# Two weight pairs held in PSUM: group 2's seventh chunk in place of group 1's

## The chip, the cores and the metric

The kernel runs on one core of a Trainium2 chip. The metric is the device time of one execution in microseconds. The kernel before takes 2106.07 us, the median of three runs (2104.05 to 2109.13).

## The reference

Two independent results stand side by side in the output. Part A is a gated long convolution over 2048 positions and 1024 channels: a short shift filter on k, a product with v, a convolution of length 2048 through the FFT, and a product with q. Part B is a transformer layer with a recurrent memory, and it takes most of the time:

```python
for s in range(64):                                   # 64 segments of 32 rows
    h = concat(mem, x[32*s : 32*s + 32])              # 8 + 32 rows, 1024 wide
    q, k, v = h @ Wq, h @ Wk, h @ Wv                  # 32 heads of 128
    p = softmax(masked(q @ k.T * 128 ** -0.5))        # mem rows see everything, the others the past
    o = (p @ v) @ Wo
    mem, out[s] = o[:8], o[8:]
```

Each segment needs the memory rows of the one before. The segments are therefore run in order, and every segment passes over all four weight matrices, 8 MB each in bfloat16.

## The kernel before, in words

**Preparation.** Up to about 388 us the kernel computes part A, and it also computes q, k and v of the 8 last rows of every segment, which the loop of part B reads back. In the loop, 32 rows (8 memory rows and 24 of x) go through the weights.

**Pairs.** The weights of part B are cut into 64 pairs of 512 KB, each [128, 2, 1024]. `("qk", g, i)` is the i-th of eight chunks of the model dimension for head group g of four, with Wq and Wk side by side. `("v", G, i)` is the same for one half of Wv, and `("o", g, i)` is two heads of Wo. In the text they are written qk0/2, v0/3 and o2/3; counting starts at 0, so group 2's seventh chunk is qk2/6 and the values' sixth chunk is v0/5.

Most pairs stay in on-chip memory for the whole loop (tiles `Wearly`, `Wqk`, `Wv`, `Wop`, `Wlate`, `Wo`). The table `STREAM` (line 40) names 17 pairs that do not fit and are loaded again in every segment. Two further pairs are kept in PSUM as bfloat16, in the tiles `park`. The table `PARKED` (line 41) names them as its values.

**The ring.** Streamed and parked pairs are used from a ring of five buffers, `wring`. When the matmuls of a ring pair have been written, `done` (line 768) gives its place to something new. Normally that is `place` (line 686): the next streamed pair in the order of use is loaded by a DMA on SP's queue (line 691). If the consumed pair is a key of `PARKED`, the place goes to the parked pair instead, and the copy is put on a list. `unpark` (line 759) then writes the copies of that list into the programs of two engines: one half on ACT (line 762), one on DVE (line 763). So the call of `unpark` sets behind which ACT and DVE work the copies stand. All places are tracked by semaphores: the load or the copy starts when the old pair's matmuls have ended.

**One segment**, in the order written out by hand (lines 948 to 1032), as PE runs it:

- q and k of group 0 (`qk_part`, line 787); in it, after chunk 4, the first `unpark`
- v chunks 0 to 3 of the first half (`v_part`, line 803), group 0's transposes (`tr_a`, line 825), then `unpark`
- q and k of group 1, chunks 0 to 3; `scores` and `softmax` of group 0; chunks 4 to 7
- v chunks 4 to 7 of the first half, group 1's transposes, `v_out` (line 814: ACT copies the values out of PSUM into `vsb`)
- q and k of group 2, with scores and softmax of group 1 in the middle; `pv` (line 896: probabilities times values) of group 0
- the same for group 3, then v of the second half with the remaining scores and softmaxes
- `wo` (line 911) of groups 0 to 3 with `pv` of groups 2 and 3 between them; the memory rows of the result, transposed, become the next segment's `hT`

Each softmax is a chain that alternates between DVE and ACT: `mx` and the subtraction on DVE (lines 866, 867), two exponentials on ACT (875, 876), sum, reciprocal, product, transpose on DVE (879 to 884), and four copies into `PB` (`blocks`, line 887).

**Queues.** All loads of the ring stand on SP's queue in the order of the calls of `place`, with the load of the next segment's `qkb`. POOL's queue has the outputs and two small loads, ACT's queue the next rows of x. After the loop the last output rows are computed in one pass (lines 1034 to 1052).

Of the kernel before, what the change touches and what calls it, by code (L numbers as in the profile page):

```python
# [21 lines left out]
def fused_kernel(ctx: ExitStack, tc, q, k, v, shift_k, ssm_k, ssm_D, outa, x, mem0, Wq, Wk, Wv, Wo, outb, n_seg):  # L22
# [14 lines left out]
    NS = 17  # L37
    scale = 128.0 ** -0.5
    RING = 5
    STREAM = {"qk": ((2, 4), (3,), (2, 6), (2, 6)), "v": ((0, 3, 5), (1, 5)), "o": ((2,), (1,), (0, 3), (2,))}  # L40
    PARKED = {("qk", 0, 4): ("v", 0, 2), ("v", 0, 3): ("qk", 1, 6)}

    msched = tc.manual_schedule()
    msched.__enter__()
# [10 lines left out]
    def keys(m, g, r):  # L55
        return [(m, g, i) for i in r]
# [3 lines left out]
    pairs += [key for g in range(4) for key in keys("o", g, range(4))]  # L60
    streamed = [key for key in pairs if key[2] in STREAM[key[0]][key[1]]]
    parked = list(PARKED.values())
    resident = [key for key in pairs if key not in streamed and key not in parked]
# [49 lines left out]
    def res_half(key, n):  # L113
        if key not in res:
            if key in early:
                res[key] = wide["t"][:, early.index(key)]
            else:
                res[key] = res_pool[key].tile([128, 2, 1024], BF, name=f"W{key[0]}{key[1]}_{key[2]}")
        nc.sync.dma_start(res[key][:, n, :], half_src(key, n))
        return res[key][:, n, :]  # L120
# [580 lines left out]
    def load_h(s):  # L701

        H_ = acte.tile([128, 256], BF, tag="qks", name="H")
        if s == 0:
            nc.gpsimd.dma_start(H_[0:32, :], mem0.rearrange("t (dq c) -> (t dq) c", dq=4))
            nc.gpsimd.dma_start(H_[32:128, :], x[0:24].rearrange("t (dq c) -> (t dq) c", dq=4))
        else:
            nc.scalar.dma_start(H_[:], x[32 * s - 8:32 * s + 24].rearrange("t (dq c) -> (t dq) c", dq=4))
        return H_
# [49 lines left out]
    def unpark():  # L759
        while to_copy:  # L760
            key, t = to_copy.pop(0)
            nc.scalar.copy(t[:, 0, :], park[key][0][:])  # L762
            nc.vector.tensor_copy(t[:, 1, :], park[key][1][:])  # L763
# [4 lines left out]
    def done(key):  # L768
        if key in res:
            return  # L770
        if key in PARKED:
            t = ring.tile([128, 2, 1024], BF, tag="wring", name="wring")
            placed[PARKED[key]] = [t[:]]
            to_copy.append((PARKED[key], t))
        else:
# [11 lines left out]
    def qk_part(u, kcs):  # L787
        if kcs[0] == 0:
            u.qk = ps_a.tile([128, 512], F32, tag="a", name="qkacc")
        for kc in kcs:  # L790
            w = pair(("qk", u.g, kc))
            for t in range(2):
                for c2 in range(2):
                    p0 = 32 * (2 * t + c2)
                    nc.tensor.matmul(u.qk[p0:p0 + 32, :], lhsT=hT[:, kc, :], rhs=w[:, t, c2 * 512:(c2 + 1) * 512],  # L795
                                     start=(kc == 0), stop=(kc == 7), tile_position=(0, p0))
            done(("qk", u.g, kc))

    def qk_out(u):
        u.qks = acte.tile([128, 512], BF, tag="qks", name="qks")  # L800
        nc.scalar.copy(u.qks[:], u.qk[:])  # L801

    def v_part(G_, kcs):
        if kcs[0] == 0:
            vacc[0] = ps_a.tile([128, 512], F32, tag="a", name="vacc")
        for kc in kcs:
            w = pair(("v", G_, kc))
            for c in range(4):
                nc.tensor.matmul(vacc[0][32 * c:32 * c + 32, :].rearrange("p (n x) -> p n x", n=2), lhsT=hT[:, kc, :],  # L809
                                 rhs=w[:, :, c * 256:(c + 1) * 256], start=(kc == 0), stop=(kc == 7),  # L810
                                 tile_position=(0, 32 * c))
            done(("v", G_, kc))

    def v_out():
        v = act.tile([128, 2, 256], BF, tag="vsb", name="vsb")
        nc.scalar.copy(v[:].rearrange("p n x -> p (n x)"), vacc[0][:])  # L816
        return v

    def transposes(src):
        tp = ps_ts.tile([128, 512], BF, tag="ts", name="tp")  # L820
        for j in range(4):
            nc.tensor.transpose(tp[:, j * 128:(j + 1) * 128], src[:, j * 128:(j + 1) * 128], ident[:])  # L822
        return tp

    def tr_a(u):
        tp = transposes(u.qks)
        tv = tp[:].rearrange("e (j t c r) -> e t c j r", j=4, t=2, c=2)
        QK = acte.tile([128, 8, 72], BF, tag="qks", name="QK")
        u.QT, u.KT = QK[:, :, 0:32], QK[:, :, 32:72]
        nc.gpsimd.tensor_copy(u.KT[:, :, 32:40], u.qkb.rearrange("e (h t r) -> e t h r", h=8, t=2)[:, 1])  # L830
        nc.scalar.copy(u.QT.rearrange("e (c j) r -> e c j r", c=2), tv[:, 0])  # L831
        nc.scalar.copy(u.KT[:, :, 0:32].rearrange("e (c j) r -> e c j r", c=2), tv[:, 1])
# [6 lines left out]
    def new_u(g):  # L839
        u = G()  # L840
        u.g = g
        u.qkb = qkb[:, g, :]
        return u
# [43 lines left out]
    def blocks(u, by):  # L887
        for c in range(4):
            r = slice(32 * c, 32 * c + 32)
            to, src = PB[r, :, c, :], u.PT[r, :, 0:40]  # L890
            if by[c] == "A":
                nc.scalar.copy(to, src)
            else:
                (nc.vector if by[c] == "D" else nc.gpsimd).tensor_copy(to, src)  # L894
# [45 lines left out]
    def new_hT():  # L940
        return acte.tile([128, 8, 32], BF, tag="hT", name="hT")
# [6 lines left out]
    for s in range(n_seg):  # L948
        last = s + 1 == n_seg
        def first_loads(g):  # L950
            for key in (n_o[g - 1:g] if s == 0 and g else ()):
                for n in range(2):
                    res_half(key, n)

        first_loads(0)
        us = [new_u(g) for g in range(4)]
        u0, u1, u2, u3 = us
        qk_part(u0, range(0, 5))
        unpark()
        qk_part(u0, range(5, 8))  # L960
        qk_out(u0)
        v_part(0, range(0, 4))
        tr_a(u0)
        unpark()
        first_loads(1)
        qk_part(u1, range(0, 4))
        S = scores(u0)
        softmax(u0, S)
        if s == 0:
            nc.vector.memset(PB[:], 0.0)  # L970
        blocks(u0, "DDDD")
        qk_part(u1, range(4, 8))
        qk_out(u1)
        v_part(0, range(4, 8))
        tr_a(u1)
        u0.v = u1.v = v_out()
        first_loads(2)
        qk_part(u2, range(0, 4))
        S = scores(u1)
        softmax(u1, S)  # L980
        if last:
            spare = [key for key in resident if key[0] != "o" and key[1] < 1 + (key[0] == "qk") and key not in early]
            for key, at in zip([key for key in streamed if key[0] == "o"], spare):
                nc.sync.dma_start(res[at][:], Wst[key])
                res[key] = res[at]
            for s0, s1 in ((0, 32), (32, s)):
                nc.sync.dma_start(OLs[:, s0:s1].rearrange("e s h r -> e (s h r)"),
                                  OLd[:, s0:s1].rearrange("e s x -> e (s x)"))
        qk_part(u2, range(4, 8))
        qk_out(u2)  # L990
        pv(u0, s)
        blocks(u1, "DDDD")
        first_loads(3)
        qk_part(u3, range(0, 2))
        tr_a(u2)
        qk_part(u3, range(2, 6))
        S = scores(u2)
        softmax(u2, S)
        qk_part(u3, range(6, 8))
        qk_out(u3)  # L1000
        v_part(1, range(0, 1))
        pv(u1, s)
        blocks(u2, "DDDD")
        v_part(1, range(1, 2))
        tr_a(u3)
        v_part(1, range(2, 5))
        S = scores(u3)
        if not last:
            H = load_h(s + 1)
            qkb = load_b(s + 1)  # L1010
        softmax(u3, S)
        v_part(1, range(5, 8))
        u2.v = u3.v = v_out()
        Y = ps_a.tile([128, 512], F32, tag="a", name="yacc")
        wo(u0, Y)
        pv(u2, s)
        blocks(u3, "DDAA")
        wo(u1, Y)
        wo(u2, Y)
        pv(u3, s)  # L1020
        if not last:
            hT = new_hT()
            h_rows(H, hT, 8)
        wo(u3, Y)
        Y_sb = act.tile([128, 256], BF, tag="P", name="Y_sb")
        nc.scalar.copy(Y_sb[:], Y[:, 0:256])  # L1026
        if not last:
            fill_mem(hT, Y_sb)
        for dq in range(4):
            nc.gpsimd.dma_start(outb[32 * s:32 * s + 24, dq * 256:(dq + 1) * 256], Y_sb[32 * dq + 8:32 * dq + 32, :])  # L1030
        if not last:
            load_vb(s + 1)
# [88 lines left out]
```

## Time and profile before

| | |
|---|---|
| median of three runs | 2106.07 us |
| the profiled execution's own time | 2093.32 us |
| its span, first to last instruction | 2091.5 us |
| granted clock of PE, mean over the span | 0.984 |
| PE busy | 1702.4 us (81%) |
| DVE, ACT, POOL busy | 1115.3, 908.7, 413.1 us |
| moved by DMA | 728.64 MB, mean 348 GB/s |
| loop of part B | about 388 to 2002 us of the span |
| one ring load, issue to landing (shortest, median, longest) | 4.0, 6.4, 9.4 us |
| copy of half a parked pair | 0.69 us on DVE, 1.02 us on ACT |

The page shows one execution. Times are counted in microseconds from the first instruction. A row of the timeline gives the start, the duration, the engine, the line of the kernel, the operation, the tile written and the tiles read. In square brackets stand the idle time of the engine just before and what ended it. PE's busy share says little by itself, since the ends of its pipelined matmuls are modelled. The share of busy time is also an average over stages with different limits, so the loop is read by single segments.

### The profile page before, as it was taken

What the parts mean: (1) busy time and instruction counts of PE and PEld (TensorE: products, weight loads), DVE (VectorE), ACT (ScalarE), POOL (GpSimd) and SP (SyncE); (2) the same over time, 40 slices, a digit from 0 to 9 for tenths busy, and PEclk for the clock granted to TensorE, in tenths of its full rate; (3) what the DMA queues carried; (4) which work ended last, traced back from release to release, by engine and by line L of the source; (5) the groups of instructions that cost most, each with busy time, mean ns of one, the idle gap of its engine ahead of it and who ended that gap; (6) DMA issues with size and microseconds to landing.
All of it is one profiled execution on the core that took longest, in us unless ns stands there. A gap on an engine that the chain in (4) does not pass through costs nothing. (4 is left out here: it accounts for less than half of the span.)

```text
span 2091.5 us, 73911 instructions
## 1 busy us (share of the span) xinstructions
PE 1702.4 (81%) x30484; PEld 894.2 (43%) x30514; DVE 1115.3 (53%) x3313; ACT 908.7 (43%) x2276; POOL 413.1 (20%) x1018
## 2 busy tenths in 40 slices
PE   5888987888788888888887878888888878888879
PEld 2433233444444444444444444444444444444449
DVE  6986833355555555555555555555555555555541
ACT  5556731244444444444444444444444444444430
POOL 2004730121111111111111111111212121111110
PEclk9999999999999999999999999999999999999999
DMA  6899989999999999999999999999999999999980
GB/s 236 282 346 362 343 287 381 352 377 372 356 375 368 365 360 370 372 366 375 358 368 353 367 358 372 359 377 358 371 358 378 363 352 351 374 370 379 368 337 23
DMA packets 266384, 728.64 MB, mean 348 GB/s; under 512 B 65007, under 2 KB 77183, under 8 KB 265277
## 3 DMA queue, kind: packets, MB, share of 16 engines
q1 hardware_dynamic: 239486, 686.65, 88.8%
q0 software_dynamic: 15520, 22.06, 3.3%
q10 hardware_dynamic: 11040, 15.21, 2.1%
q8 instruction: 239, 3.92, 0.7%
q14 instruction: 99, 0.81, 0.1%
HBM read 673.52 MB, written 56.56 MB: 349 GB/s over the span
## 5 line engine op out<-in xcount | busy, mean ns | idle before, releaser
L795 PE MATMUL qkacc<-Wqk,hT 128*32 128x512 bf16 x4096 | 338.5, 383 | 0.0
L795 PEld LDWEIGHTS <-hT 128*32 128x32 bf16 x8192 | 184.9, 96 | 236.3 <-issue 84.2
L916 PEld LDWEIGHTS <-OT 128*32 128x32 bf16 x8192 | 210.1, 96 | 109.5 <-issue 59.2
L795 PE MATMUL qkacc<-wring,hT 128*32 128x512 bf16 x2048 | 204.9, 389 | 31.3 <-DMA wring<-Wstqk 25.5
L763 DVE COPY wring<-park 128x1024 bf16<-128x1024 bf16 x128 | 88.6, 692 | 239.4 <-PE vacc L809 124.8
L875 ACT ACTIVATE P<-S 128x128 bf16<-128x128 f32 x256 | 71.1, 278 | 330.4 <-DVE S L867 244.3
L809 PE MATMUL vacc<-Wv,hT 128*32 128x512 bf16 x2560 | 209.8, 382 | 0.0
L809 PE MATMUL vacc<-wring,hT 128*32 128x512 bf16 x1536 | 154.7, 387 | 65.5 <-DMA wring<-in_B_Wv_dram 63.6
L809 PEld LDWEIGHTS <-hT 128*32 128x32 bf16 x4096 | 113.0, 95 | 184.4 <-issue 108.3
L762 ACT COPY wring<-park 128x1024 bf16<-128x1024 bf16 x128 | 130.7, 1021 | 138.9 <-PE qkacc L795 112.8
L894 DVE COPY PB<-P 32x160 bf16<-32x160 bf16 x896 | 172.9, 193 | 10.6
L879 DVE TENSOR_REDUCE sm<-P 128x4 f32<-128x256 bf16 x256 | 107.5, 420 | 128.6 <-ACT P L876 128.6
L831 ACT COPY QK<-tp 128x256 bf16<-128x256 bf16 x256 | 95.4, 373 | 185.7 <-PE tp L822 184.5
L795 PE MATMUL qkacc<-Wearly,hT 128*32 128x512 bf16 x2048 | 161.0, 391 | 18.4 <-DVE hT L936 17.9
L830 POOL COPY QK<-qkb 128x64 bf16<-128x64 bf16 x256 | 61.3, 239 | 564.5 <-PE tp L822 404.8
L916 PE MATMUL yacc<-wring,OT 128*32 128x256 bf16 x2520 | 126.7, 274 | 37.4 <-DMA wring<-Wsto 35.2
L905 ACT CAST OT<-otacc 128x256 bf16<-128x256 f32 x256 | 98.7, 386 | 130.4 <-PE otacc L901 130.4
L801 ACT CAST qks<-qkacc 128x512 bf16<-128x512 f32 x256 | 151.1, 590 | 4.2 <-PE qkacc L795 3.5
L1030 POOL DMA_DIRECT2D out_dram<-Y_sb x256 | 129.1, 511 | 84.8 <-ACT Y_sb L1026 82.8
L822 PE MATMUL tp<-ident,qks 128*128 128x128 bf16 x1024 | 102.4, 223 | 52.6 <-ACT qks L801 50.3
L866 DVE TENSOR_REDUCE mx<-S 128x4 f32<-128x160 f32 x256 | 83.2, 325 | 85.2 <-PE S L863 79.5
L901 PE MATMUL otacc<-PB,vsb 128*128 128x160 bf16 x512 | 97.6, 238 | 35.3 <-ACT vsb L816 35.3
(212 smaller groups left out, 2957.1 us busy)
## 6 DMA issues: line engine op xcount, KB each, us to landing
wring<-Wstqk SPq DMA_DIRECT2D x448, 512.0 KB, 6.2
wring<-in_B_Wv_dram SPq DMA_DIRECT2D x320, 512.0 KB, 6.7
wring<-Wsto SPq DMA_DIRECT2D x315, 512.0 KB, 6.3
SK<-s_sb SPq DMA_DIRECT2D x8, 1024.0 KB, 5.5
SU<-s_sb SPq DMA_DIRECT2D x8, 1024.0 KB, 8.9
QKBd<-stq ACTq DMA_DIRECT2D x4, 2048.0 KB, 9.5
Kg<-SK SPq DMA_DIRECT2D x16, 512.0 KB, 7.0
Ug<-SU SPq DMA_DIRECT2D x16, 512.0 KB, 8.3
```

Source lines behind the costliest of these rows:

```text
L762: nc.scalar.copy(t[:, 0, :], park[key][0][:])
L795: nc.tensor.matmul(u.qk[p0:p0 + 32, :], lhsT=hT[:, kc, :], rhs=w[:, t, c2 * 512:(c2 + 1) * 512], start=(kc == 0), stop=(kc == 7), tile_pos ...
L801: nc.scalar.copy(u.qks[:], u.qk[:])
L809: nc.tensor.matmul(vacc[0][32 * c:32 * c + 32, :].rearrange("p (n x) -> p n x", n=2), lhsT=hT[:, kc, :], rhs=w[:, :, c * 256:(c + 1) * 256 ...
L822: nc.tensor.transpose(tp[:, j * 128:(j + 1) * 128], src[:, j * 128:(j + 1) * 128], ident[:])
L831: nc.scalar.copy(u.QT.rearrange("e (c j) r -> e c j r", c=2), tv[:, 0])
L879: nc.vector.tensor_reduce(out=sm[:], in_=Pv.rearrange("p b x k -> p x b k"), op=ALU.add, axis=AX.XY)
L894: (nc.vector if by[c] == "D" else nc.gpsimd).tensor_copy(to, src)
L901: nc.tensor.matmul(o, lhsT=w[:, i * 128:(i + 1) * 128], rhs=PB[:, 2 * kb + i].rearrange("p c q -> p (c q)"), start=(kb == 0), stop=(kb == 1))
L905: nc.scalar.copy(u.OT[:].rearrange("e (c i) q -> e i c q", i=2), ov[:, :, :, 0:32])
L916: nc.tensor.matmul(Y[32 * dq:32 * dq + 32, 0:256], lhsT=u.OT[:, hh, 0:32], rhs=w[:, hh % 2, dq * 256:(dq + 1) * 256], start=(u.g == 0 and ...
L1030: nc.gpsimd.dma_start(outb[32 * s:32 * s + 24, dq * 256:(dq + 1) * 256], Y_sb[32 * dq + 8:32 * dq + 32, :])
```

## The change

Group 1's seventh chunk, qk1/6, which was kept in PSUM, becomes a streamed pair. Group 2's seventh chunk, qk2/6, which was streamed, is kept in PSUM. The number of streamed and of parked pairs stays the same. The parked pair's copy now takes the place of v0/5 in the ring (before, that of v0/3), and its `unpark` stands behind group 1's transposes (before, behind group 0's).

```diff
-    STREAM = {"qk": ((2, 4), (3,), (2, 6), (2, 6)), "v": ((0, 3, 5), (1, 5)), "o": ((2,), (1,), (0, 3), (2,))}
-    PARKED = {("qk", 0, 4): ("v", 0, 2), ("v", 0, 3): ("qk", 1, 6)}
+    STREAM = {"qk": ((2, 4), (3, 6), (2,), (2, 6)), "v": ((0, 3, 5), (1, 5)), "o": ((2,), (1,), (0, 3), (2,))}
+    PARKED = {("qk", 0, 4): ("v", 0, 2), ("v", 0, 5): ("qk", 2, 6)}
...
         v_part(0, range(0, 4))
         tr_a(u0)
-        unpark()
         first_loads(1)
         qk_part(u1, range(0, 4))
...
         v_part(0, range(4, 8))
         tr_a(u1)
+        unpark()
         u0.v = u1.v = v_out()
```

The order in which pairs of the ring are used is the same before and after: qk0/2, qk0/4, v0/0, v0/2, v0/3, qk1/3, qk1/6, v0/5, qk2/2, qk2/6, qk3/2, qk3/6, v1/1, v1/5, o0/2, o1/1, o2/0, o2/3, o3/2.

## The prediction, as it was made before the result

> **What bounds the kernel now.** I read the first page, then the windows by stage, then the ring's tile `wring`, then the timeline of one loop iteration, engine by engine. The page gives the span and the transfers; its last line here is the DMA share of the 40 slices:
>
> ```profile
> span 2091.5 us, 73911 instructions
> ...
> DMA  6899989999999999999999999999999999999980
> ...
> q1 hardware_dynamic: 239486, 686.65, 88.8%
> ```
>
> The windows by stage (engine columns, then granted PE clock, DMA share, GB/s); the 64 segments run from 388 to 2002:
>
> ```profile
> 388.00:2002.00 1614.00, 1312.85 (x27468) 698.46 (x27469) 845.11 (x2900) 709.74 (x1954) 307.63 (x880) 0.99 0.99 366
> 906.00:907.00 1.00, 0.88 (x36) 0.50 (x32) 0.11 (x1) 1.00 (x2) 0.00 (x0) 1.00 0.81 322
> 908.00:909.00 1.00, 0.91 (x20) 0.31 (x16) 0.80 (x3) 0.58 (x3) 0.00 (x0) 1.00 1.04 418
> 910.00:911.00 1.00, 1.00 (x39) 0.35 (x29) 0.85 (x4) 0.26 (x1) 0.20 (x1) 1.00 0.90 332
> 911.00:912.00 1.00, 0.97 (x16) 0.34 (x12) 0.49 (x2) 0.56 (x3) 0.00 (x0) 1.00 0.89 328
> ```
>
> What to see: 1614 us over 63 steps is 25.6 us a segment, with the DMA engines at 0.99, yet short stretches at 0.81 to 0.90. The loop is bound by its stream of 17 pairs of 512 KB, with little to spare. PE still waits for it, as the ring's own view says:
>
> ```profile
>   PE vacc L809: 63.6, 121
>   PE yacc L916: 35.2, 72
>   PE qkacc L795: 25.5, 45
> ...
> DMA to landing us min/median/max: 4.0/6.4/9.4
> ```
>
> Together 124.3 us, 1.97 us a segment. Last, one ordinary segment (901.10 to 926.34), PE, then SP, DVE, ACT:
>
> ```profile
> 903.35 0.40 PE L809 MATMUL vacc<-wring,hT 128*32 128x512 bf16 x4 [0.34 <-DMA wring<-in_B_Wv_dram]
> 904.62 0.40 PE L809 MATMUL vacc<-wring,hT 128*32 128x512 bf16 x4 [0.44 <-DMA wring<-in_B_Wv_dram]
> 906.24 0.40 PE L795 MATMUL qkacc<-wring,hT 128*32 128x512 bf16 x4
> 907.06 0.40 PE L795 MATMUL qkacc<-wring,hT 128*32 128x512 bf16 x4
> 907.70 0.40 PE L809 MATMUL vacc<-wring,hT 128*32 128x512 bf16 x4
> ```
>
> ```profile
> 901.98 0.33 SPq L691 DMA_DIRECT2D wring<-in_B_Wv_dram  x1
> 903.79 4.07 SPq L691 DMA_DIRECT2D wring<-Wstqk  x4
> 908.15 2.02 SPq L691 DMA_DIRECT2D wring<-in_B_Wv_dram  x2
> ```
>
> ```profile
> 905.07 0.69 DVE L763 COPY wring<-park 128x1024 bf16<-128x1024 bf16 x1 [1.96 <-PE vacc L809]
> 909.74 0.82 DVE L894 COPY PB<-P 32x160 bf16<-32x160 bf16 x4
> 910.59 0.33 DVE L866 TENSOR_REDUCE mx<-S 128x4 f32<-128x160 f32 x1
> ```
>
> ```profile
> 905.98 1.03 ACT L762 COPY wring<-park 128x1024 bf16<-128x1024 bf16 x1
> 909.65 0.60 ACT L816 CAST vsb<-vacc 128x512 bf16<-128x512 f32 x1
> ```
>
> The PE rows are, in order, v0/0, v0/3, qk1/3, qk1/6 (today from PSUM) and v0/5. SP issues right behind a consumed pair: 901.98 follows the first streamed pair (901.54, 0.39 long), 903.79 follows v0/0. So a consumed pair's place takes the next load, and the ring always looks five pairs ahead.
>
> **The change, part by part.** *Amounts.* 17 streamed pairs and two PSUM copies remain, of the same shapes; preparation moves as many bytes. Cost 0, but only the order of that stage's relayed pairs changes, so +-1 us.
>
> *The order of loads.* Today the places freed by qk0/2, v0/0, v0/2, qk1/3, qk1/6, v0/5 are loaded with v0/5, qk2/2, qk2/6, qk3/2, qk3/6, v1/1; v0/3's takes the copy. Afterwards qk0/2, v0/0, v0/2, v0/3, qk1/3, qk1/6 give qk1/6, v0/5, qk2/2, qk3/2, qk3/6, v1/1, and v0/5's place takes the copy of qk2/6. From qk2/2's place on the loads are the same. So at the issue of 901.98, which now brings v0/5 for 907.70, qk1/6 is fetched for 907.06; and v0/5 goes out at 903.79, 3.91 us ahead of its use. v0/5's head start falls from 5.72 to 3.91 us.
>
> *The stall.* The trace's shortest landing is 4.0, its median 6.4 us. Bounds: 903.79 + 4.0 = 907.8, a stall of 0.1 us; 903.79 + 6.4 = 910.2, 2.5 us. The nearest rows are the landings just ahead: v0/0 released PE at 903.35, v0/3 at 904.62, and qk1/3 is in by 906.24, steps of 1.27 and 1.62, mean 1.45. Two more steps put qk1/6 at 907.7 and v0/5 at 909.1: PE late by 0.6, then 1.4 us in all. The same moments averaged over segments 4 to 59 of the trace, from each segment's start: the two issues land at 6.91 and 8.53, the uses are at 6.54 and 7.25, 1.3 us late. I take 1.3.
>
> The Trainium skill, "DMA: Bandwidth & Descriptors", section on the anatomy of one DMA, fits a transfer as about 2.0 us plus bytes over 436 GB/s (for the gpsimd path). That estimate for 512 KB is 3.2 us, so v0/5 would come at 907.0 and never be late; the 4.0 us minimum disagrees, and the sum would then be only the copy's, below.
>
> *What the stall gives back.* The stream keeps running while PE stands, so later waits shrink. They are 1.97 us a segment, so all 1.3 could come back (0 net, if the engines stay busy) or nothing (+1.3). In the after order five pairs are in flight or in place when PE stands at v0/5; the next issue comes only behind qk2/2 (its matmuls start at 909.40 in the same timeline; + 0.40 + 1.3 = 911.1), while today one goes out at 908.15. From the last issue behind qk1/6 (907.06 + 0.40 + 0.6 = 908.1) that is a gap of 3.0 us without an issue. At the mean step of 1.45 the pairs in flight, qk2/2, qk3/2, qk3/6, v1/1, land at 910.5, 912.0, 913.4 and 914.9, so the next load, due at 916.3, must land by then to lose nothing; 911.1 + 4.0 = 915.1 makes it with 1.2 us over. Today's median landing of 6.4 has 2.4 over the shortest. Half the cover is gone. The steps between landings vary: of 690 neighbouring pairs in the trace about half are within 0.03 of 1.28 us and a quarter over 1.59, and four of the fast ones use up 0.7 of the 1.2 (4 x 0.17). Worked on the same way for the next six loads, from the averaged uses that free their places (9.04, 10.26, 12.30, 13.45, 14.66 and 16.98, each + 0.4 + 1.3 + 4.0, against due times from 15.8 in steps of 1.45), the margin is 1.0, 1.2, 0.7, 1.0, 1.2 and 0.3. So it is positive but thin all along, nearer to the end where all comes back: I take 0.9 of 1.3, leaving +0.4 us a segment, ends 0 and 1.3.
>
> *The copies.* Today's pair of copies (DVE 0.69, ACT 1.03) stands behind group 0's transposes in idle time; removing it wins 0, as the first softmax waits for S anyway. Behind group 1's, DVE has PB to 910.56 and then mx at 910.59: the copy pushes that chain by 0.69 us if S is on time, but S is 1.3 us late, so it runs in the stall's shadow: 0 beside it, 0.69 if the cover goes. On ACT it stands ahead of vsb: 909.65 becomes 910.7 + 0.6 = 911.3, while pv (L901) starts at 910.97 in that timeline: PE waits 0.3 to 0.4 more, which I count inside the range, for PE waits for ACT's qks at tr_a(u2) soon after. Copy ready: 911.8 at worst (+1.3 counted), its use in group 2, today at 910.43, + 1.3 = 911.7: 0 to 0.1. Queued behind the copies are softmax(u1), qks of u2 and all that follows; no queue of POOL's is passed, and SP passes only the reordered loads.
>
> *Sum.* 0.4 us x 63 = +25 us, with 2 for the pv wait: +27. The profiled execution took 2093.32 us (span 2091.5 and 1.8 around it), giving 2120; it lies 12.75 below the median of 2106.07, so 2133 for the median.
>
> **Rivals.** *Rate-bound, no change.* DMA share 0.99 says any order costs the same. Against: share is full only because issues come early enough. 2106. The Trainium skill, same page, section on where 436 GB/s comes from, has about 358 GB/s per core bind for HBM loads; by it 366 is already the limit and nothing could change. The 418 GB/s of 908 to 909 speaks against such a limit here.
>
> *Faster.* The load moved from 908.15 to behind v0/3 (905.0) fills the thin stretches: missing shares at 906, 910 and 911 are 0.19 + 0.10 + 0.11 = 0.40 us; half won is 0.2 x 63 = -13 us, 2093. It decides if qk1/6 and v0/5 land within 5.1 and 3.9 us of their issue; the 4.0 us minimum is against it.
>
> *No stall, but the copy in the chain.* If the stall goes, DVE's 0.69 delays every later softmax; PE waits for that chain at pv(u2) already. 0.69 x 63 = +43, 2149.
>
> *Nothing comes back.* 1.3 x 63 = +82, 2188. For it: PE's chain after scores(u1) is tight (mx follows PB by 0.03 us). Against: 1.97 us of waits are there to shrink.
>
> **How the numbers follow.** Forecast 0.48, copy in the chain 0.12, nothing back 0.15: slower 0.75. Rate-bound: same 0.14. Faster 0.11. About 0.2% (4 us) is what this kernel's runs can tell. The likeliest case alone spans +8 to +60 us, 2114 to 2166. The range reaches from 2098 (part of the faster case) to 2180 (short of nothing back), leaving under 2 in 10 out.
>
> **What would show it.** After: a new wait of PE at qk1/6 and v0/5, together 0.8 to 1.4 us a segment, with v0/0, v0/3 and L916's waits below today's; DMA share in the segments 0.97 to 0.98; the second L763 copy directly between PB and mx. Wrong, if v0/5 shows no wait, if the segments stay at 25.6 us with PE's new wait taken wholly from old ones, or if the share rises to 1.00.

## The result, and the profile after

The changed kernel takes 2198.87 us, the median of six runs (2183.58 to 2208.94); the kernel before, run beside it, 2104.41 us. The ratio is 1.0469 with a 95% interval of 1.0420 to 1.0518. The change costs about 94 us. The forecast was 2133 us with a range of 2098 to 2180, so the direction was right and the size was missed.

The first page of the changed kernel, its span, the DMA share of its 40 slices and its main queue:

```profile
span 2199.8 us, 73975 instructions
...
DMA  6899999999999999999999999999999999999990
...
q1 hardware_dynamic: 239486, 686.65, 86.7%
```

The same bytes pass over the same queue, and the page's digits still show 9 all along. The windows show more. First the whole loop, then stretches of one ordinary segment (start 1038.00, length 26.95 us), as duration, busy time of PE, PEld, DVE, ACT and POOL, granted PE clock, DMA share, GB/s:

```profile
388.00:2105.00 1717.00, 1339.30 (x27421) 695.17 (x27414) 842.82 (x2896) 713.70 (x1952) 301.80 (x877) 0.97 0.96 343
1044.00:1047.00 3.00, 1.30 (x24) 0.56 (x23) 1.98 (x6) 0.97 (x3) 0.21 (x1) 1.00 0.83 283
1047.00:1050.00 3.00, 2.88 (x65) 1.22 (x58) 1.94 (x7) 2.22 (x6) 0.38 (x2) 1.00 1.03 421
1052.00:1053.00 1.00, 1.00 (x41) 0.40 (x32) 0.90 (x4) 0.01 (x1) 0.20 (x1) 1.00 0.84 266
1053.00:1054.00 1.00, 0.78 (x12) 0.35 (x8) 0.45 (x2) 0.51 (x3) 0.00 (x0) 1.00 0.90 291
```

The share over the loop went from 0.99 to 0.96 and the rate from 366 to 343 GB/s. The engines now run thin twice in a segment, while PE waits (1044 to 1047) and again around 1052. Who waited for the ring's tile `wring` (us in total, times), and the landing times:

```profile
  PE vacc L809: 133.8, 165
...
  PE qkacc L795: 46.8, 71
  PE yacc L916: 32.5, 56
...
DMA to landing us min/median/max: 3.8/6.4/9.5
```

The waits of the value matmuls went from 63.6 to 133.8 us and those of q and k from 25.5 to 46.8. The waits in `wo` (L916) hardly moved, 35.2 to 32.5. In the segment from 1038.00, the timeline of PE shows v0/0, v0/3, qk1/3, qk1/6 and v0/5, and that of SP the issues:

```profile
1040.28 0.40 PE L809 MATMUL vacc<-wring,hT 128*32 128x512 bf16 x4 [0.37 <-DMA wring<-in_B_Wv_dram]
...
1041.54 0.40 PE L809 MATMUL vacc<-wring,hT 128*32 128x512 bf16 x4 [0.43 <-DMA wring<-in_B_Wv_dram]
...
1042.96 0.40 PE L795 MATMUL qkacc<-wring,hT 128*32 128x512 bf16 x4
...
1044.64 0.40 PE L795 MATMUL qkacc<-wring,hT 128*32 128x512 bf16 x4 [0.68 <-DMA wring<-Wstqk]
...
1046.53 0.40 PE L809 MATMUL vacc<-wring,hT 128*32 128x512 bf16 x4 [1.06 <-DMA wring<-in_B_Wv_dram]
```

```profile
1040.72 0.33 SPq L691 DMA_DIRECT2D wring<-in_B_Wv_dram  x1
1041.22 2.50 SPq L691 DMA_DIRECT2D wring<-Wstqk  x3
1045.08 3.75 SPq L691 DMA_DIRECT2D wring<-in_B_Wv_dram  x2
```

v0/5 is issued at 1040.72, behind v0/0, and used at 1046.53, 5.8 us later. PE stands still before qk1/6 and again before v0/5. The old waits at v0/0 and v0/3 are still there. The new place of the copies is seen on DVE:

```profile
1046.82 0.81 DVE L894 COPY PB<-P 32x160 bf16<-32x160 bf16 x4
1047.66 0.69 DVE L763 COPY wring<-park 128x1024 bf16<-128x1024 bf16 x1
1048.92 0.32 DVE L866 TENSOR_REDUCE mx<-S 128x4 f32<-128x160 f32 x1 [0.57 <-PE S L863]
```

The copy stands between PB and mx, and DVE still waits 0.57 us for the scores behind it: it is hidden.

Averaged over segments 4 to 59 of both traces, in us from each segment's start (a landing where the trace has it, which is so for 947 of 1083 loads; wait is PE's idle time just before the use):

| pair | before: landing, use, wait | after: landing, use, wait |
|---|---|---|
| qk0/2 | -0.40, 0.48, 0.01 | -0.39, 0.48, 0.00 |
| v0/0 | 2.42, 2.52, 0.36 | 2.67, 2.78, 0.42 |
| v0/3 | 3.94, 3.96, 0.60 | 4.10, 4.22, 0.56 |
| qk1/3 | 5.44, 5.51, 0.09 | 5.66, 5.78, 0.09 |
| qk1/6 | copy, 6.54, 0.04 | 7.15, 7.24, 0.46 |
| v0/5 | 6.91, 7.25, 0.02 | 9.19, 9.24, 1.15 |
| qk3/2 | 11.44, 12.30, 0.01 | 11.97, 14.17, 0.00 |
| v1/1 | 14.31, 14.66, 0.04 | 14.74, 16.35, 0.00 |
| v1/5 | 16.07, 16.98, 0.00 | 16.66, 18.75, 0.00 |
| o3/2 | 23.74, 23.87, 0.23 | 25.50, 25.52, 0.38 |
| mean length of all 63 steps | 25.61 | 27.33 |

The use of v0/5 is 1.99 us later and the segment 1.72 us longer; 63 x 1.72 = 108 us, the difference of the two profiled spans (2199.8 - 2091.5). From v0/5 on only 0.3 us comes back, and about as much (0.27 us at qk1/3) is already lost ahead of the new waits. In between, pairs now lie in the ring for 2 us before their use (qk3/2, v1/5), and as long as they do, their places can take no load.

The profiled executions differ by 108 us, the medians by 94: the execution before lay 11 us under its median, the one after 3 us over. The traces also differ in PE's granted clock, 0.984 and 0.970 over the spans. It falls to 0.50 for stretches of 3.4 or 6.8 us (for example 1063.60 to 1070.40 in the changed kernel). Of segments 4 to 59, such a stretch touches 10 before and 20 after. The 46 and 36 segments without one average 25.30 and 26.77 us, and 63 times that difference is 93 us (an estimate). So the lower clock does not explain the cost; why it fell more often after the change was not tried.

### The profile page after: what moved, and what is told of

Read it like the earlier page. It is cut to its first block, busy times and chain, and to the rows that moved or that the text cites. A ratio compares the mean times of both kernels' runs of the same rounds, so it can differ in the third digit from the quotient of the medians.

```text
span 2199.8 us, 73975 instructions
## 1 busy us (share of the span) xinstructions
PE 1732.9 (79%) x30484; PEld 893.1 (41%) x30514; DVE 1114.0 (51%) x3313; ACT 913.7 (42%) x2276; POOL 408.7 (19%) x1018
## 4 chain that ended last, share of the span: by engine, by line
DMA 42%; PE 33%; DVE 12%; ACT 8%; issue 3%; POOL 0%; SPq 0%; DVEq 0%; ACTq 0%; POOLq 0%
DMA wring<-in_B_Wv_dram 32%; PE qkacc L795 10%; PE vacc L809 5%; PE yacc L916 3%; DMA wring<-Wsto 3%; PE otacc L901 3%; PE pl L1044 3%; PE tp L822 2%; ACT wring L762 2%; DVE PB L894 2%; PE ps_k L181 1%; DMA wring<-Wstqk 1%; PE ps_q L181 1%; DVE sm L879 1%; ACT vsb L816 1%
## 5 line engine op out<-in xcount | busy, mean ns | idle before, releaser
L795 PE MATMUL qkacc<-Wqk,hT 128*32 128x512 bf16 x4096 | 346.3, 391 | 0.0
L809 PE MATMUL vacc<-wring,hT 128*32 128x512 bf16 x1536 | 158.8, 403 | 134.0 <-DMA wring<-in_B_Wv_dram 133.8
L795 PE MATMUL qkacc<-wring,hT 128*32 128x512 bf16 x2048 | 210.9, 399 | 55.3 <-DMA wring<-Wstqk 46.5
L916 PEld LDWEIGHTS <-OT 128*32 128x32 bf16 x8192 | 209.8, 96 | 102.5 <-issue 52.6
L809 PE MATMUL vacc<-Wv,hT 128*32 128x512 bf16 x2560 | 214.9, 391 | 0.0
L795 PE MATMUL qkacc<-Wearly,hT 128*32 128x512 bf16 x2048 | 168.6, 407 | 18.4 <-DVE hT L936 17.8
L916 PE MATMUL yacc<-wring,OT 128*32 128x256 bf16 x2520 | 126.2, 274 | 35.4 <-DMA wring<-Wsto 32.5
```

Source lines behind the costliest of these rows:

```text
L916: nc.tensor.matmul(Y[32 * dq:32 * dq + 32, 0:256], lhsT=u.OT[:, hh, 0:32], rhs=w[:, hh % 2, dq * 256:(dq + 1) * 256], start=(u.g == 0 and ...
```

## The experiments

Two theories stood at first. **Order**: the new order of the loads alone costs the time, and the copies are hidden behind the wait. **Copies**: the copies in their new place delay `vsb`, `pv` and the second softmax. All kernels below were run beside the kernel before on the same chip, and the ratio is to that.

### The copies replaced by a fill on POOL

```diff
         while to_copy:
             key, t = to_copy.pop(0)
+            if key == ("qk", 2, 6):
+                nc.gpsimd.memset(t[:], 0.0)
+                continue
```

> The changed kernel, but the two copies of qk2/6 on ACT and DVE are replaced by one fill with zeros on POOL, into the same place of the ring at the same point of the program (so group 2 works with zeros for this pair). Order theory: the 94 us come from the order of the loads alone, the copies stand in the shadow of the wait at v0/5; the time stays within 10 us of the changed kernel (about 2190 to 2200). Copy theory: the copies delay vsb, pv of group 0 and the second softmax by 0.7 to 1.0 us in each of 63 segments; 45 to 65 us faster than the changed kernel, about 2135 to 2155.

Measured: 2217.80 us, ratio 1.0555 (1.0496 to 1.0614), 19 us slower than the changed kernel. ACT and DVE are rid of these copies and nothing is won, against the copy theory, which had 45 to 65 us less. The order theory's 2190 to 2200 was missed too. The fill itself is no clean replacement: the trace has it at 1.80 us on POOL, and PE now waits 0.53 us a segment before qk2/6 (0.10 in the changed kernel). 0.43 x 63 = 27 us of the time is that wait. Without it the time would be near 2191, where the order theory had it; this is an estimate, since no run has the copies gone and nothing in their place.

### v0/5 used two pairs later

```diff
-        v_part(0, range(4, 8))
+        v_part(0, (4, 6, 7, 5))
```

The matmul that ends the sum is then chunk 5's.

> The changed kernel, but the last four value chunks of the first half are used in the order 4, 6, 7, 5, so that v0/5 is needed two resident pairs (0.43 us) later; nothing else moves. Order theory: what is short is the time between the freeing of v0/0's place and the use of v0/5, so the wait at v0/5 shrinks by about 0.4 us and 63 segments give 20 to 27 us back (about 2172 to 2180). Copy theory: the copies start 0.4 us later than before relative to the transposes, so 0 to 10 us slower than the changed kernel.

Measured: 2169.12 us, ratio 1.0330 (1.0269 to 1.0391), 30 us less than the changed kernel. By the ratios that is 1.4%, or 0.46 us a segment (the two intervals leave 16 us, or 0.26 us a segment, either way), and the use was moved by 0.43. The wait at v0/5 fell from 1.15 to 0.62 us on average. Within that error the head start comes back in full. Had 0.9 of every 1.3 us of stall returned elsewhere, as the prediction had it, only 0.43 x 0.4 / 1.3 x 63 = 8 us would have been won.

### The new set of pairs with the copies in their old place

```diff
-    PARKED = {("qk", 0, 4): ("v", 0, 2), ("v", 0, 5): ("qk", 2, 6)}
+    PARKED = {("qk", 0, 4): ("v", 0, 2), ("v", 0, 3): ("qk", 2, 6)}
...
         tr_a(u0)
+        unpark()
...
         tr_a(u1)
-        unpark()
```

> Half of the change: qk1/6 is streamed and qk2/6 kept in PSUM, but the copy still takes v0/3's place and still stands behind group 0's transposes. Order theory: qk1/6 and v0/5 come out of the same places as in the changed kernel, so the wait at the two stays (0.4 and 1.1 us); in addition the place of v0/3 is held by the copy from about 4 to 12 us, so the loads qk3/2, qk3/6 and v1/1 go out one use later: as slow as the changed kernel or slower, 2190 to 2260. Copy theory: the copies are back in their old idle time, so most of the 94 us comes back, 2105 to 2130.

Measured: 2184.98 us, ratio 1.0394 (1.0337 to 1.0451). The waits at qk1/6 and v0/5 stay (0.48 and 0.93 us), and so does most of the loss. So the place of the copies is at most a small part of the cost. That this kernel came out 14 us below the changed kernel lies at the edge of what the two intervals can tell.

### One load fewer, in two ways

In the changed kernel the load of qk1/6 was left out, and in the kernel before that of qk2/6; the matmuls read a resident chunk instead.

```diff
+    LEFT = {("qk", 1, 6): ("qk", 1, 5)}     # the other kernel: {("qk", 2, 6): ("qk", 2, 5)}
...
-    streamed = [key for key in pairs if key[2] in STREAM[key[0]][key[1]]]
+    streamed = [key for key in pairs if key[2] in STREAM[key[0]][key[1]] and key not in LEFT]
...
     def pair(key):
+        key = LEFT.get(key, key)
```

> The changed kernel without the load of qk1/6: its matmuls read the resident qk1/5 instead, so 16 pairs are streamed and qk1/6 has no place in the ring; the copies of qk2/6 stay where the change has them. Order theory: v0/5 gets back its head start, the wait at qk1/6 and v0/5 goes, and the loop is back at the kernel before or under it, since one transfer of 1.3 to 1.5 us is gone as well: 2060 to 2110. Copy theory: the copies still delay the second softmax; not below 2140.

> The kernel before without the load of qk2/6 (its matmuls read the resident qk2/5): 16 loads as in the changed kernel without qk1/6, but the second pair of copies is the early one, qk1/6 into v0/3's place behind group 0's transposes. That other kernel took 2134 us; its difference to this one is the price of the copies in the late place where no wait hides them. Copies cost 0.45 us a segment (read from its trace between qk2/2 and qk3/2): this one 28 us or more below it, 2060 to 2105. Copies cost nothing: 2125 to 2140.

Measured: the changed kernel without qk1/6 takes 2134.29 us, ratio 1.0156 (1.0090 to 1.0222); the kernel before without qk2/6 takes 2093.23 us, ratio 0.9988 (0.9959 to 1.0017). Two things follow, and neither theory had both.

The second kernel moves 6% fewer bytes in its loop and gains nothing. Its share and rate over most of the loop:

```profile
390.00:2000.00 1610.00, 1299.18 (x27328) 691.62 (x27320) 840.23 (x2888) 707.05 (x1949) 305.53 (x877) 0.98 0.96 345
```

The rate fell to 345 GB/s instead of the time. So the kernel before was not bound by the bytes, although its DMA share was 0.99. The main waits stayed: 0.36 us at v0/0 (0.36 before), 0.57 at v0/3 (0.60), and 0.44 at o3/2 (0.23).

The first kernel missed its expectation: with the same number of loads it is slower than the second by 0.0168 of the ratio, 35 us (about 15 either way, from the two intervals). In its trace 3.71 us pass between the uses of qk2/2 and qk3/2, in the other's 3.19. This is where the late copies stand. In the changed kernel itself the same stretch takes 3.22 us, before 3.26. So the late copies seem to cost about 0.5 us a segment when nothing else holds PE, and nothing where PE comes late anyway. The two kernels also differ in which uses free the places of qk3/2, qk3/6 and v1/1, so this is the likely cause and not an isolated one.

### Six and seven places

```diff
-    RING = 5
+    RING = 6                                # and 7
+    LEFT = {("qk", 2, 7): ("qk", 2, 5)}     # with 7: qk2/7 and qk2/5, which read qk2/4
...
```

The pairs left out are resident ones and make room in memory, so the loop's loads stay the same. `LEFT` works as above. Two theories are set against each other. **Places**: a load can go out no earlier than the use that frees its place, so more places mean more head start. **Rate**: the transfers are the limit, and more places bring next to nothing.

> The kernel before with six places in the ring; the memory for it comes from the resident pair qk2/7, which is left out (its matmuls read qk2/5), so the loop moves the same 17 loads. Theory of places: a load can be no earlier than the use that frees its place, so one place more gives every load some 1.4 us more head start, and PE's waits for the ring (1.97 us a segment) shrink to what the transfer rate leaves: 2040 to 2090. Rate theory: the engines are at 0.99, so no more than 1% is to be had: 2080 to 2105.

> The changed kernel with six places, made in the same way. Theory of places: v0/5 is then loaded into a place freed one use earlier, its wait goes, and the difference to the kernel before with six places falls from 95 us to under 30 us. If instead the copies behind group 1's transposes are the cost, or the transfers as such, the difference stays at 60 us or more.

> The kernel before with seven places; the memory comes from two resident pairs, qk2/5 and qk2/7, which are left out (their matmuls read qk2/4). 17 loads as before. Theory of places: with six places the DMA engines are already at 1.00 of the loop, so the transfers themselves are the bound and a seventh place brings little: 2000 to 2025 against 2022.

> The changed kernel with seven places, made in the same way. Theory of places: the order of the loads costs only as far as a load can't be sent early enough; the difference went from 95 us (five places) to 47 us (six), so with seven it goes to 0 to 20 us, at 2005 to 2040. If part of the 47 us is another cost (the copies in the late place, 41 us in the pair of kernels with 16 loads), the difference stays at 30 us or more.

Measured:

| places | before | after | difference of the ratios |
|---|---|---|---|
| 5 | 2104.41 | 2198.87 | 4.7%, 94 us |
| 6 | 2022.31, ratio 0.9634 (0.9603 to 0.9666) | 2069.70, ratio 0.9862 (0.9816 to 0.9909) | 2.3%, 48 us |
| 7 | 2032.81, ratio 0.9688 (0.9652 to 0.9724) | 2056.46, ratio 0.9795 (0.9764 to 0.9826) | 1.1%, 22 us |

The half-widths of the intervals, taken together, leave about 12 us on the second difference and 10 on the third. Each place more about halves the cost of the change. Both differences lie between what was expected of places alone (under 30 us with six, 0 to 20 with seven) and of another cost beside them (60 or more, 30 or more). A sixth place is worth 3.7% to the kernel before as well, more than either theory had expected, and a seventh nothing more. What is left with seven places shows in who waits for the ring there. First the kernel before, then the changed one:

```profile
  PE vacc L811: 1.1, 3
  PE qkacc L797: 0.8, 1
```

```profile
  PE vacc L811: 38.3, 54
  PE qkacc L797: 24.2, 73
```

With seven places the kernel before waits for loads 1.9 us in all, next to nothing, and a segment takes 24.58 us. The changed one takes 25.06. It still waits at v0/5 (use at 6.63 instead of 5.86 us after the start), but of that 0.77 only 0.27 is left at qk2/2. Between qk2/2 and qk3/2 it then takes 3.76 instead of 3.31 us: the copies' price of 0.45 again. The remaining 22 us thus seem to hold both, the loads and the copies. How much is which these runs don't separate.

### Other uses of the same 17 loads

If the crowd of loads at the segment's start is the whole cause, thinning it should help. Three kernels do it. In the first, qk1/3 is resident and qk2/4 streamed in the changed kernel. The second has in addition the copies back in the old place. The third makes the same exchange in the kernel before.

```diff
-    STREAM = {"qk": ((2, 4), (3, 6), (2,), (2, 6)), ...
+    STREAM = {"qk": ((2, 4), (6,), (2, 4), (2, 6)), ...
```

> The changed kernel, but qk1/3 is resident and qk2/4 is streamed in its stead: 17 loads and the changed copies as they are, but six instead of seven loads are used between the segment's start and v0/5. Theory of crowding (the ring brings one pair per 1.4 to 1.6 us, and the places hold no more than five ahead): the wait of 1.6 us at qk1/6 and v0/5 goes; what stays is the price of the late copies where nothing hides them, 0.4 to 0.65 us a segment: 2100 to 2140. If the change costs through something else than the crowding, it stays near 2199.

> The same set of pairs, but the copies of qk2/6 stand behind group 0's transposes again and go into v0/3's place, as the copies of qk1/6 did before the change. Against the kernel with the late copies: copies cost 0.4 to 0.65 us a segment where no wait hides them, so 20 to 40 us less; but the place of v0/3 is held from about 4 to 11 us, which takes a place from the loads of group 3 and can eat 0 to 20 us of it: 2085 to 2120. Copies cost nothing: equal or slower than with the late copies.

> The kernel before, but qk1/3 is resident and qk2/4 streamed in its stead: five loads instead of six are used up to v0/5, the same 17 in all. Theory of crowding alone: PE's waits at v0/0 and v0/3 (1.0 us a segment) are set by loads issued in the segment before and stay, so only the 0.1 us at qk1/3 goes, and one load more stands in group 2, where landing and use lie 0.3 to 0.5 us apart: 2085 to 2115, no clear gain. If the number of loads up to v0/5 were all that counts, 1.4 us a segment less for the uses up to there: 2040 to 2070.

Measured: 2159.43 us (ratio 1.0290, 1.0241 to 1.0339), 2160.63 us (1.0290, 1.0239 to 1.0342) and 2160.87 us (1.0309, 1.0271 to 1.0347). The wait at qk1/6 and v0/5 does go in the first, from 1.61 to 0.22 us, but only 39 us come back. Part of the rest is an accident of these three, at the end of the program. In the last segment the first kernel shows, on SP and then on PE:

```profile
2067.51 1.49 SPq L984 DMA_DIRECT2D Wv<-Wsto  x1
2069.05 2.56 SPq L984 DMA_DIRECT2D Wqk<-Wsto  x4
2071.78 1.25 SPq L987 DMA_DIRECT2D Wearly<-OLd  x2
2073.14 0.61 SPq L691 DMA_DIRECT2D wring<-in_B_Wv_dram  x1
```

```profile
2091.06 0.62 PE L809 MATMUL vacc<-wring,hT 128*32 128x512 bf16 x4 [15.61 <-DMA wring<-in_B_Wv_dram]
```

The load of v1/5 now stands behind the block of large transfers for the final pass, and PE waits 15.6 us for it. From the last segment's start to the end these kernels take 101 to 103 us against 90. In the profiled executions the other 49 to 58 us are in the loop, 0.8 to 0.9 us a segment: new waits turn up at qk2/4 (0.3 us in the first two), at v1/1 (0.14 to 0.48), at o2/0 (0.21 to 0.39) and at o2/3 (0.46 to 0.67, in the kernel before 0.26). The third kernel has the early copies and no load of qk1/6, and it is just as slow. So the waits moved to other uses. The expectation that only the segment's start is short was wrong: in the kernel before, the loads from v0/5 to o2/0 land only 0.3 to 1.1 us before their use, all along the segment. That the second equals the first leaves two readings: the late copies cost nothing here, or they cost as much as holding v0/3's place longer, as the early copies do. No run separates these.

The last one moves a use instead of a load, in the kernel before:

```diff
-        v_part(0, range(0, 4))
+        v_part(0, (0, 1, 2, 4))
...
-        v_part(0, range(4, 8))
+        v_part(0, (3, 6, 7, 5))
```

with the loads in that order and qk1/6 copied into v0/2's place.

> The kernel before with the uses of the first half's value chunks in another order: 0, 1, 2, 4 ahead of group 1 and 3, 6, 7, 5 behind it, so v0/3 is needed some 2.5 us later; qk1/6 is copied into v0/2's place. The set of loads, the copies and their stage stay as they are. Theory of places: the loads at the start of a segment come too late for uses that lie too close; v0/3's wait (0.6 us a segment) mostly goes, and v0/0's stays: 10 to 35 us faster than before, 2070 to 2095. Rate theory: no change, 2095 to 2110.

Measured: 2113.43 us, ratio 1.0082 (1.0047 to 1.0118), slower by a little, where the places theory had expected a gain and the rate theory no change. v0/3's wait is gone (0.60 to 0.01), and waits grow at qk2/6 (0.09 to 0.33), at v0/5 (0.02 to 0.21) and at o2/3 (0.26 to 0.49). No other order or choice of 17 loads in five places that was tried beat the kernel before. The versions with more places do, but a further place was had only by leaving out weights.

## Why the prediction was right or wrong

**The order of the loads: right.** The waits moved to qk1/6 and v0/5 as foreseen, and v0/5 is issued behind v0/0.

**The stall: right in kind, too small.** Predicted 1.3 us at v0/5, measured 1.99 later than before, of which 0.27 was already there at qk1/3; so 1.72 is new. v0/5 landed at 9.19 us instead of the 8.53 taken over from the old trace. The load ahead of it, now qk1/6, landed 0.24 us later (7.15 for 6.91), and from it to v0/5 the step was 2.04 us, not 1.62. The Trainium skill's fit for one DMA ("DMA: Bandwidth & Descriptors", anatomy of one DMA, there for the gpsimd path) gives an estimate of 3.2 us for 512 KB and would have shown no stall. In the changed kernel's trace the shortest landing was 3.8 us and the median 6.4; over all runs the shortest was 3.2 us, in the last kernel above.

**What the stall gives back: this step failed.** 0.9 of 1.3 us were to return through shorter waits at later uses. Measured, v0/0 waits 0.42 instead of 0.36, v0/3 0.56 instead of 0.60, and `wo` 32.5 us in all instead of 35.2. The working showed only that the loads after the stall would still be in time; from that I took it that the stream runs ahead meanwhile. It does so only as far as five places reach. v1/1 lands just 0.43 us later than before, although v0/5 was used 1.99 us later; but its place and the others stay taken until PE uses their pairs. The next loads wait for these late uses, and the lead is lost again: v1/5 lands 0.59 us later than before, o1/1 1.06, o3/2 1.76 (it is issued 1.78 us later and takes 6.0 us to its landing in both traces). The loads for the next segment's start are issued behind the last uses of this one, at the same distance from its end (qk0/2 at -6.93 us instead of -7.01, v0/0 at -4.48 instead of -4.52). They come no earlier to the next start: qk0/2 lands at -0.39 instead of -0.40, v0/0 at 2.67 instead of 2.42. A stall in the middle doesn't help them. That the places matter is shown by the cost falling by half with each place added, and the missing return by the use moved by 0.43 us, which gave 0.46.

**The cover of 1.2 us: too large.** It was counted with the shortest landing, 4.0 us. In the thin stretch after the stall, where v1/5 (11.42 to 16.66), o0/2 and o1/1 were issued, landings took 5.2 to 5.4 us. The gap without an issue ahead of v1/5 was 3.7 us (7.69 to 11.42), where 3.0 was counted. By that, the loads after the stall had nothing to spare.

**The copies: right.** 0 beside the stall was forecast and found (3.22 us against 3.26 in the stretch), and 0.69 if the cover goes; where it went, the stretch grew by 0.45 to 0.5. The 2 us for `pv` were not to be seen: PE does not wait ahead of group 0's `pv` in either trace.

**The rivals.** "Nothing comes back", 2188 us, was the right one, with 0.15. With the stall at 1.72 instead of 1.3 it gives 63 x 1.72 = 108 us, the difference of the profiled executions. That the two agree to the last digit is chance: 0.3 us does come back, 0.27 is lost ahead of the stall, and the lower clock seems to have a share. "Rate-bound" is excluded, also for the kernel before. By the Trainium skill's limit of about 358 GB/s per core for loads from HBM ("DMA: Bandwidth & Descriptors", where 436 GB/s comes from) no order could matter. The traces disagree: the loop of the kernel before with seven places ran at 382 GB/s:

```profile
390.00:1930.00 1540.00, 1261.78 (x27292) 677.49 (x27283) 841.82 (x2884) 709.33 (x1946) 304.86 (x876) 0.99 1.01 382
```

**Signs named beforehand.** The copy between PB and mx is there. The new wait at qk1/6 and v0/5 is there too, 1.61 us where 0.8 to 1.4 was named. The DMA share is 0.96, a little below the 0.97 to 0.98 named. The waits at v0/0, v0/3 and in L916 were to shrink by 0.9 us a segment and hardly moved: this is the sign that decides it.

## What to carry to other kernels

In a ring of buffers the head start of a load is counted in uses, from the one that frees its place to its own, and its price is read from the landings under the same traffic, not from the shortest one. A wait at one use was not paid back here by waits elsewhere, because the loads that end those were issued no earlier. Before calling a loop bound by bandwidth at a DMA share of 0.99, take one load away or add one buffer: here the first gained nothing and the second 3.7%.

## What the runs showed of the hardware

The DMA share says that the engines hold packets, not how fast they move them. In the changed kernel's segment two stretches of 3 us stand side by side, 1047 to 1050 with share 1.03 and 421 GB/s (above), and the next:

```profile
1050.00:1053.00 3.00, 3.00 (x68) 1.37 (x65) 2.60 (x10) 1.62 (x6) 0.44 (x2) 1.00 0.98 315
```

A share near 1 thus went with rates a quarter apart. Why transfers take longer in some stretches was not tried.
